# A third weight buffer and one-by-one loads at the start of an MLP, in place of a split store queue and copies on VectorE at its end

## The chip, the cores and the metric

The kernel runs on one core of a Trainium2 chip. A core has five engines that run side by side, each with its own instruction stream: TensorE (PE in the profile) multiplies matrices, VectorE (DVE) and ScalarE (ACT) work element by element, GpSimd (POOL) does the same and issues software transfers, and SyncE (SP) issues most transfers between the off-chip memory (HBM) and the on-chip memory (SBUF). Matmul results land in PSUM, from where VectorE or ScalarE fetch them. An engine executes its instructions in their order: when one of them waits, all behind it wait too. The metric is the device time of one execution in microseconds; lower is better.

## The reference

Attention with a hashed mask, followed by an MLP with a parametric ReLU. There are 4 batches, 8 heads, 768 positions, head size 64; the MLP has 3072 rows, a model size of 512 and a hidden size of 2048. All inputs and outputs are float32.

```python
def _attn_ref(q, k, v, proj):
    q_bits = (np.einsum('bhsd,dk->bhsk', q, proj) > 0).astype(np.int64)
    k_bits = (np.einsum('bhsd,dk->bhsk', k, proj) > 0).astype(np.int64)
    q_bucket, k_bucket = ...            # the 6 bits of each as a number
    mask = q_bucket[:, :, :, None] == k_bucket[:, :, None, :]
    scores = np.where(mask, scale * np.matmul(q, k.transpose(0, 1, 3, 2)), -1e9)
    attn = np.exp(scores - np.max(scores, axis=-1, keepdims=True))
    attn = attn / (np.sum(attn, axis=-1, keepdims=True) + 1e-09)
    return np.matmul(attn, v)

def _moe_ref(x, w_in, w_out, alpha):    # x: attention's output, heads side by side, (3072, 512)
    h = x @ w_in                        # w_in  (512, 2048)
    g = np.maximum(h, 0.0) + alpha * np.minimum(h, 0.0)
    return g @ w_out                    # w_out (2048, 512)
```

## The kernel before

The kernel first runs attention in 32 units (16 pairs of heads, two halves of the queries each). While it does, it rounds the MLP's weights, forms sums of blocks of w_in, and stores both in HBM (w_in_s, w_out_r). Then come 4 batches of the MLP, each with 8 blocks of the first product (called f_0 to f_7) and 7 of the second (z_1, z_2, z_5, z_6, z_3, z_7, z_4, in this order).

Both products use Winograd's form of Strassen's method: seven products of sub-blocks in place of eight, at the price of sums before and after. The class `Product` makes one block. Its steps 1, 2, 22, 5, 6, 3, 7, 4 are seven products in three PSUM banks (a, b, c); `keep` copies a bank to SBUF on ScalarE before more is added on top of it, and `finish` makes a quarter of the result ("11", "12", "22", "21") on VectorE.

```python
    def load_w(n):                       # w_in's blocks for f_n
        if n < B * NI:
            w_m[n] = mid.tile([P, NM, 2, P], F32, name=f"wi{n}", tag="wi")   # the pool has bufs=2
            nc.sync.dma_start(w_m[n], w_in_s[n % NI])

    class Product:
        ...
        def keep(self, bank, what):
            t = mid.tile([P, CW], F32, name=f"{self.name}{what}", tag=what, bufs=1)[:, : self.width]
            do(ACT.copy(t, self.ps[bank]))
            self.sb[what] = t

        def step(self, n):
            if n == 1:
                self.times("a", 0, 0, True)
                self.keep("a", "p1")
            elif n == 2:
                self.times("b", 1, 1, True)
            elif n == 22:
                self.kept("11", self.sb["p1"])
                self.finish("11", self.sb["p1"], self.ps["b"])
            elif n == 5:
                self.times("c", 3, 3, True)
                self.keep("c", "p5")
            elif n == 6:
                self.times("a", 4, 4, False)
                self.keep("a", "u1")
                self.kept("22", self.sb["p5"])
                self.kept("12", self.sb["u1"])
            elif n == 3:
                self.times("c", 6, 2, False)
                self.finish("12", self.sb["u1"], self.ps["c"])
            elif n == 7:
                self.times("a", 5, 5, False)
                self.keep("a", "u2")
                self.finish("22", self.sb["p5"], self.sb["u2"])
            elif n == 4:
                self.times("a", 2, 6, False)
                self.finish("21", self.ps["a"], None)
```

Here `times("a", ...)` of step 6 adds onto bank a, so it has to wait for the copy of p1 that step 1 began. `do` keeps an instruction in program order on its engine; transfers without `do` are placed by the scheduler.

During the first batch, w_out's sums are formed too, 8 groups of them, read from w_out_r and stored to w_out_s by transfers that GpSimd issues:

```python
    def load_out(n):
        if n < NI:
            t = late[0].tile([P, 2, 4, DM // 2], F32, name=f"wo{n}", tag="wl")
            for i in range(2):
                nc.gpsimd.dma_start(t[:, i], w_out_r[:, :, n + i].rearrange("m p d -> p m d"))
                w_o[n + i] = t[:, i]

    def sum_out(n):
        w = w_o[n]
        for to, x, op, y in (...):       # four sums
            do(DVE.tensor_tensor(w[:, to], w[:, x], w[:, y], op=op))
        nc.gpsimd.dma_start(w_out_s[:, :, n].rearrange("m p d -> p m d"), w)
        if n % 2:
            load_out(n + 3)
```

The finished parts of the output are transposed on VectorE and stored (`turn_out`), except the last two parts, which go through TensorE (`turn_last`):

```python
    def turn_out():
        while to_turn:
            ...
            for i in range(2):
                do(DVE.transpose(o[:, :, i], m2[b, p][:, i]))
            for a in range(DM // 128):           # 4
                for c in range(CH):              # 3
                    (nc.scalar if b == B - 1 and p == 3 and c % 2 else nc.sync).dma_start(...)

    def turn_last(n):
        ...
        if n == 0:
            ...                                  # six transposes, two copies on ScalarE, one store
            return
        ps = cells("tx", [(0, 0), (1, 0)])       # TensorE transposes
        ps2 = cells("ty", [(2, 0), (2, 1)])
        do(DVE.tensor_copy(o[:, :, :, 0], ps))
        do(ACT.copy(o2.rearrange("p f i -> p i f"), ps2))
        nc.scalar.dma_start(dst[:, 2], o2.rearrange("p f i -> p (f i)"))
        do(DVE.tensor_copy(o[:, :, :, 1], cells("tz", [(0, 1), (1, 1)])))
        nc.sync.dma_start(dst[:, :2], o.rearrange("p t f i -> p t (f i)"))
```

The loop over the blocks, cut to what the steps need:

```python
    load_out(0)
    load_out(2)
    for j, (b, what, n) in enumerate(blocks):
        ...                                      # steps 2, 22, 5, 6, 3, 7 of this block, and sums for the next
        if j == 4:
            verdict()                            # is every input within the fast path's range?
        for n_out in [(), (0,), (1,), (2,), (3, 4), (5,), (6, 7)][j] if j < 7 else ():
            sum_out(n_out)
        if what == "1":
            load_w(b * NI + n + 2)
            ...
        if j + 1 < len(blocks):
            turn_out()
        else:
            turn_last(0)
        before = now
        if j + 1 < len(blocks):
            now = ...                            # the next block
            now.step(1)
        before.step(4)
        ...
    turn_last(1)
```

Of the kernel before, what the change touches and what calls it, by code (L numbers as in the profile page):

```python
# [406 lines left out]
def fast_path(  # L407
# [59 lines left out]
    qbs = [const.tile([P, S], BF16, name=f"qb{i}") for i in range(2)]  # L467
# [36 lines left out]
    def setup():  # L504

        zero = const.tile([P, 512], BF16, name="zero")
        do(DVE.memset(zero, 0.0))
        do(DVE.memset(wh, 0.0))
        for s in range(2):
            nc.sync.dma_start(wh[D * s : D * s + D, :NB], proj)  # L510
        nc.sync.dma_start(alpha16, moe_alpha.rearrange("(t p) -> t p", p=P))
        make_identity(nc, ident)
        do(DVE.memset(ones, 1.0))

        ps = psum.tile([P, 512], F32, name="nil", tag="av")
        nil.append(lambda: do(PE.matmul(ps, zero[:, :P], zero, start=True, stop=True)))
        for i in range(7):
            nil[0]()

        do(DVE.memset(hb, 0.0))  # L520
        for r in range(0, P, 32):
            do(DVE.memset(hb[r : r + 2 * NB], 1.0 if r % D else -1.0))
            do(DVE.memset(hb[r : r + NB], -1e-37))

        do(DVE.tensor_scalar(hb_k[:, 0:1], hb, -1.0, None, op0=ALU.mult))
        do(DVE.memset(hb_k[:, 1:2], 0.0))
        for r in range(0, P, 32):
            do(DVE.memset(hb_k[r : r + 2 * NB, 1:2], 0.5))
        for t in pts:
            do(POOL.memset(t[:, :, CW : CW + 1], 1.0))  # L530
        for t in qbs:
            do(POOL.memset(t, 0.0))
# [296 lines left out]
    def load_w(n):  # L829

        if n < B * NI:
            w_m[n] = mid.tile([P, NM, 2, P], F32, name=f"wi{n}", tag="wi")
            nc.sync.dma_start(w_m[n], w_in_s[n % NI])

    class Product:
# [3 lines left out]
        def __init__(self, name, width, nk, left, right, finish, kept=None):  # L839
            self.name, self.width, self.nk = name, width, nk  # L840
            self.kept = kept if kept else lambda c, t: None
            self.left, self.right, self.finish = left, right, finish
            self.ps, self.sb = {}, {}
# [21 lines left out]
        def step(self, n):  # L865
# [5 lines left out]
            elif n == 22:  # L871
                self.kept("11", self.sb["p1"])
# [4 lines left out]
            elif n == 6:  # L877
                self.times("a", 4, 4, False)
                self.keep("a", "u1")
                self.kept("22", self.sb["p5"])  # L880
                self.kept("12", self.sb["u1"])
# [56 lines left out]
    def load_out(n):  # L938

        if n < NI:  # L940
            t = late[0].tile([P, 2, 4, DM // 2], F32, name=f"wo{n}", tag="wl")
            for i in range(2):
                nc.gpsimd.dma_start(t[:, i], w_out_r[:, :, n + i].rearrange("m p d -> p m d"))
                w_o[n + i] = t[:, i]

    def sum_out(n):

        w = w_o[n]
# [3 lines left out]
        if n % 2:  # L952
            load_out(n + 3)
# [24 lines left out]
    def ff2(b, n):  # L978
# [11 lines left out]
        def finish(c, x, more):  # L990
            i, jj = int(c[0]) - 1, int(c[1]) - 1
            dst = acc[:, i, jj * HC : (jj + 1) * HC]
            if p == 4:

                do(DVE.tensor_tensor(dst, m2[b, 1][:, i, jj * HC : (jj + 1) * HC] if more is None else dst, x if more is None else more, op=ALU.add))
            elif more is not None:
                do(DVE.tensor_tensor(dst, x, more, op=ALU.add))
            else:
                do(ACT.copy(dst, x))
# [8 lines left out]
        def kept(c, x):  # L1008
            i, jj = int(c[0]) - 1, int(c[1]) - 1
            m = m2[b, 1][:, i, jj * HC : (jj + 1) * HC]  # L1010
            do(DVE.tensor_tensor(acc[:, i, jj * HC : (jj + 1) * HC], x, m, op=ALU.add))

        return Product(
            f"z{b}_{p}", HC, HK, lambda m, k: w2[b, n, m][:, k], lambda m, k: g2[b, n, m][:, k], finish,
            kept if p == 4 else None,
        )

    def turn_out():
        while to_turn:
# [6 lines left out]
            for a in range(DM // 128):  # L1026
                for c in range(CH):
                    cols = slice(half * DM // 2 + 64 * a, half * DM // 2 + 64 * a + 64)

                    (nc.scalar if b == B - 1 and p == 3 and c % 2 else nc.sync).dma_start(  # L1030
# [4 lines left out]
    def turn_last(n):  # L1035


        b, p, half, ch = to_turn.pop(0)
        dst = out_v[b, ch * CH : (ch + 1) * CH].rearrange("c p d -> p c d")[:, :, half * 2 * P : (half + 1) * 2 * P]

        def cells(name, at):
            ps = two_banks(f"{name}{p}")[:, 0].rearrange("p (t f) -> p t f", f=P)
            for k, (t, i) in enumerate(at):
                do(PE.transpose(ps[:, k], m2[b, p][:, i, t * P : (t + 1) * P], ident))
            return ps[:, : len(at)]

        if n == 0:
            o = late[0].tile([P, CH, P, 2], F32, name=f"o_{p}", tag="o")
            for i in range(2):
                do(ACT.copy(o[:, :, :, i], cells(f"to{i}", [(t, i) for t in range(CH)])))  # L1050
            nc.sync.dma_start(dst, o.rearrange("p t f i -> p t (f i)"))
            return
        o = late[0].tile([P, 2, P, 2], F32, name=f"o_{p}", tag="o")
        o2 = late[0].tile([P, P, 2], F32, name=f"o2_{p}", tag="m5", bufs=1)
        ps = cells("tx", [(0, 0), (1, 0)])
        ps2 = cells("ty", [(2, 0), (2, 1)])
        do(DVE.tensor_copy(o[:, :, :, 0], ps))
        do(ACT.copy(o2.rearrange("p f i -> p i f"), ps2))
        nc.scalar.dma_start(dst[:, 2], o2.rearrange("p f i -> p (f i)"))
        do(DVE.tensor_copy(o[:, :, :, 1], cells("tz", [(0, 1), (1, 1)])))  # L1060
        nc.sync.dma_start(dst[:, :2], o.rearrange("p t f i -> p t (f i)"))
# [3 lines left out]
    col = const.tile([32, 32], F32, name="col")  # L1065
    row = const.tile([32, 32], F32, name="row")

    def largest():
        do(DVE.memset(col, 0.0))
# [4 lines left out]
    def verdict():  # L1074
        ps = psum.tile([4, P], F32, name="vd", tag="sm")
        do(PE.transpose(ps, top, ident))
        do(DVE.tensor_reduce(col[:4, 0:1], ps, axis=mybir.AxisListType.X, op=ALU.max))
        do(DVE.transpose(row, col))
        do(DVE.tensor_tensor(row[0:1, 0:1], row[0:1, 0:1], row[0:1, 1:2], op=ALU.mult))

        do(DVE.tensor_scalar(row[0:1, 0:1], row[0:1, 0:1], SAFE, None, op0=ALU.is_le))
        do(DVE.tensor_scalar(row[0:1, 2:3], row[0:1, 2:3], HI_END, None, op0=ALU.is_lt))
        do(DVE.tensor_scalar(row[0:1, 3:4], row[0:1, 3:4], 1.0, None, op0=ALU.is_le))
        do(DVE.tensor_tensor(row[0:1, 0:1], row[0:1, 0:1], row[0:1, 2:3], op=ALU.mult))
        do(DVE.tensor_tensor(row[0:1, 0:1], row[0:1, 0:1], row[0:1, 3:4], op=ALU.mult))
        do(DVE.tensor_scalar(flag, row[0:1, 0:1], -1.0, 1.0, op0=ALU.mult, op1=ALU.add))
# [37 lines left out]
    for u in range(UNITS):  # L1124
# [37 lines left out]
        if u == HW + 2:  # L1162
            load_w(0)
            load_w(1)
            load_x(0)
        if HW + 4 <= u < HW + 8:
            sum_x(0, u - HW - 4, DVE)
# [15 lines left out]
    load_out(2)  # L1183
# [3 lines left out]
    for j, (b, what, n) in enumerate(blocks):  # L1187
# [25 lines left out]
        if j == 4:  # L1213
            verdict()
        for n_out in [(), (0,), (1,), (2,), (3, 4), (5,), (6, 7)][j] if j < 7 else ():
            sum_out(n_out)
        if what == "1":
            load_w(b * NI + n + 2)
# [52 lines left out]
```

## Time and profile before

| | us |
|---|---|
| time, median of 3 runs | 907.64 (906.12 to 910.24) |
| span of the profiled execution | 908.5 |
| attention with the weights' rounding | to about 346 |
| first batch of the MLP | about 346 to 486 |
| batches 2 to 4 | about 135 each |
| end of the last matmul, start of the last store's issue | 900.8, 901.28 |

A line of the profile gives busy time, share of the span and number of instructions of an engine. The chain of waits is followed back from the last instruction, at each step to what released it. The names of the pieces are the program's: `f_2a` is bank a of block f_2, `wi` are w_in's blocks in SBUF, `wl` are w_out's, `m` is a block of the second product's result, `z_4p` is a kept copy of block z_4, `ACTq` and `SPq` are the transfers that ScalarE and SyncE issue. Batch numbers are left out of the names. A busy TensorE is not TensorE at its peak, since matmuls are pipelined. A granted clock below 1 (`PEclk`, in tenths) means that TensorE's pulses were throttled.

### The profile page before, as it was taken

How to read it: one execution, taken by the hardware profiler on the slowest of the kernel's cores; microseconds unless marked ns; L12 is line 12 of the kernel's file. 1: busy time of each engine (PE TensorE's matmuls, PEld its weight loads, DVE VectorE, ACT ScalarE, POOL GpSimd, SP SyncE). 2: the span in 40 equal slices, each digit the busy share in tenths (PEclk: the TensorE clock that was granted, in tenths of full speed). 3: DMA queues.
4: the chain of work that ended last, by engine and by line, in shares of the span. 5: the costliest groups of instructions: out<-in, count | busy, mean ns of one | idle time of the engine just before them, and what ended most of it. 6: DMA issues, size and time to landing. Idle time of an engine off the chain costs nothing.

```text
span 908.5 us, 15657 instructions
## 1 busy us (share of the span) xinstructions
PE 890.3 (98%) x5882; PEld 593.7 (65%) x5882; DVE 755.0 (83%) x1357; ACT 408.6 (45%) x731; POOL 100.6 (11%) x194
## 2 busy tenths in 40 slices
PE   8999999999999999999999999999999999999995
PEld 4444454444444444557997557997557997557994
DVE  4888988988999996799889678898678898678883
ACT  6888888878888862222112222112222112222111
POOL 1222222222222231110000000000000000000000
PEclk9999999999999999999999999999999999999997
DMA  8777888698798574578334434334334434430431
GB/s 221 186 188 184 210 228 210 153 294 217 176 245 213 143 185 163 176 246 302 139 111 120 147 122 151 143 107 129 138 122 151 144 106 124 142 122 1 145 105 56
DMA packets 131909, 146.88 MB, mean 162 GB/s; under 512 B 78304, under 2 KB 118000, under 8 KB 128240
## 3 DMA queue, kind: packets, MB, share of 16 engines
q1 hardware_dynamic: 118496, 124.16, 44.0%
q0 software_dynamic: 11008, 20.97, 11.4%
q8 instruction: 48, 0.79, 0.4%
q10 hardware_dynamic: 2320, 0.66, 0.3%
q14 instruction: 37, 0.30, 0.1%
HBM read 104.87 MB, written 28.31 MB: 147 GB/s over the span
## 4 chain that ended last, share of the span: by engine, by line
PE 91%; DMA 3%; DVE 3%; issue 1%; SPq 0%; ACTq 0%; ACT 0%; DVEq 0%
PE sc L734 17%; PE av L767 14%; PE z_4a L855 2%; PE f_0a L855 2%; PE f_2a L855 2%; PE f_5a L855 2%; PE z_3a L855 2%; PE z_6a L855 2%; PE z_5a L855 2%; PE f_3a L855 2%; PE z_2a L855 2%; PE f_6a L855 2%; PE f_4a L855 2%; PE f_1a L855 2%; PE z_7a L855 2%; PE z_1a L855 2%
## 5 line engine op out<-in xcount | busy, mean ns | idle before, releaser
L739 ACT ACTIVATE pt<-sc 128x768 f32<-128x768 f32 x192 | 152.9, 814 | 46.3 <-PE sc L734 43.9
L734 PE MATMUL sc<-qT,kT 64*128 64x384 f32 x768 | 155.3, 482 | 0.0
L767 PE MATMUL av<-pt,vn 128*32 128x384 f32 (+1 forms) x1536 | 130.6, 488 | 0.0
L767 PEld LDWEIGHTS av<-pt,vn 128*32 128x32 f32 x1536 | 46.6, 109 | 75.1 <-issue 72.1
L734 PEld LDWEIGHTS sc<-qT,kT 64*128 64x128 f32 x768 | 68.2, 188 | 35.1 <-issue 34.8
L908 DVE TENSOR_TENSOR g<-g,g 128x384 f32<-128x384 f32 x128 | 68.4, 555 | 2.2
L734 PE MATMUL sc<-qb,kb 64*128 64x384 bf16 x384 | 63.4, 324 | 2.0 <-ACT kb L722 0.8
L749 POOL DMA_DIRECT2D accp<-pt x32 | 38.6, 1205 | 190.9 <-issue 86.2
L976 DVE TENSOR_TENSOR gs<-g,gs 128x768 f32<-128x768 f32 x56 | 53.4, 953 | 1.0
L968 DVE TENSOR_TENSOR ws<-wl 128x512 f32<-128x512 f32 x56 | 38.5, 688 | 18.7 <-DMA wl<-w_out_s 17.3
L976 DVE TENSOR_TENSOR gs<-g 128x768 f32<-128x768 f32 x56 | 53.3, 953 | 0.0
L904 DVE SCALAR_TENSOR_TENSOR g<-h,alpha 128x384 f32<-128x384 f32 x32 | 19.7, 617 | 27.8 <-ACT h L897 27.8
L734 PEld LDWEIGHTS <-kb 64*128 64x128 bf16 x384 | 19.4, 94 | 33.3 <-issue 11.4
L711 ACT ACTIVATE qb<-hs,hb 32x384 bf16<-32x384 f32 x62 | 35.6, 574 | 1.1
L757 DVE TENSOR_TENSOR accd<-accd,accp 128x768 f32<-128x768 f32 x32 | 30.7, 958 | 4.4 <-DMA accp<-pt 3.4
L754 DVE TENSOR_TENSOR accd<-accd,pt 128x768 f32<-128x768 f32 x32 | 30.7, 958 | 3.3
L748 DVE TENSOR_TENSOR accp<-pt,pt 128x768 f32<-128x768 f32 x32 | 30.4, 951 | 2.6 <-ACT pt L739 2.6
L753 DVE TENSOR_TENSOR accd<-pt,pt 128x768 f32<-128x768 f32 x32 | 30.4, 949 | 0.0
L803 POOL COPY rr<-rr 32x6 f32<-32x6 f32 x64 | 27.6, 432 | 2.6
L722 ACT ACTIVATE kb<-hs,hb 64x384 bf16<-64x384 f32 (+1 forms) x47 | 27.2, 579 | 0.6
L802 POOL COPY rr<-rr 32x6 f32<-32x6 f32 x64 | 19.9, 311 | 65.5 <-DVE rr L799 64.2
L797 DVE STREAM_TRANSPOSE st<-sm 128x192 f32<-128x192 f32 x32 | 12.2, 381 | 15.8 <-PE sm L779 15.7
(349 smaller groups left out, 1826.5 us busy)
## 6 DMA issues: line engine op xcount, KB each, us to landing
wi<-w_in_s SPq DMA_DIRECT2D x32, 896.0 KB, 4.8
wl<-w_out_s SPq DMA_DIRECT2D x16, 1024.0 KB, 4.8
accp<-pt POOLq DMA_DIRECT2D x32, 384.0 KB, 5.6
wl<-w_out_r SPq DMA_DIRECT2D x12, 1024.0 KB, 4.8
raw<-in_moe_w_out_dram SPq DMA_DIRECT2D x16, 512.0 KB, 5.6
raw<-in_moe_w_in_dram SPq DMA_DIRECT2D x16, 512.0 KB, 4.4
w_in_s<-wsi SPq DMA_DIRECT2D x16, 448.0 KB, 5.8
vn<-in_v_dram SPq DMA_DIRECT2D x16, 384.0 KB, 6.0
```

Of the source, the lines that this page charges most:

```text
L711: do(ACT.activation(bits["q", pi][D * s : D * s + 32, cols], ps["q"][c : c + 32, half, :CW], AF.Sign, bias=hb[c : c + 32],))
L734: do(PE.matmul(sc[:, s, :CW], what["k", pi][r, ks], what["q", pi][r, qs], start=first, stop=not first,))
L739: do(ACT.activation(pt[:, :, :CW], sc[:, :, :CW], AF.Exp, scale=SCALE / DOWN))
L748: do(DVE.tensor_tensor(accp[u], p(u, 0), p(u, 1), op=ALU.add))
L749: nc.gpsimd.dma_start(accp[u], p(u, 2), accum_op=ALU.add)
L754: do(DVE.tensor_tensor(accd[u], accd[u], p(u, 5), op=ALU.add))
L757: do(DVE.tensor_tensor(accd[u], accd[u], accp[u], op=ALU.add))
L767: do(PE.matmul(av[u][D * s + t : D * s + t + 32, :w], nat["v", pi][:, s, kc * D + t : kc * D + t + 32], prob[u, kc][:, s, :w], start=(kc = ...
L855: do(PE.matmul(self.ps[bank], self.left(left, k), self.right(right, k), start=start and k == 0, stop=k == self.nk - 1, skip_group_check=no ...
L908: do(DVE.tensor_tensor(new_g(b, to)[:, i], g_m[b, x][:, i], g_m[b, y][:, i], op=ALU.subtract))
L968: do(DVE.tensor_tensor(t, w2[b, n, x], w2[b, n, y], op=op))
L976: do(DVE.tensor_tensor(t, g2[b, n, x], g2[b, n, y], op=ALU.subtract))
```

## The change

w_in's blocks get three buffers, so that a block's weights can be asked for one block earlier; the bits of q and a zero tile move to the pool that ends with attention, which makes room. w_out's groups are loaded one by one, at fixed places of the first five blocks, where the version before loaded them in pairs, each pair from within the sums of an earlier group. In exchange, the change takes out what the version before did at the end: adding quarters of block z_4's kept copies to the result ahead of the matmuls they wait for, splitting the stores of one output part over two queues, and copying the last transposes on VectorE and ScalarE at once. The final range verdict also has another form.

```diff
-    qbs = [const.tile([P, S], BF16, name=f"qb{i}") for i in range(2)]
+    qbs = [pool.tile([P, S], BF16, name=f"qb{i}", bufs=1) for i in range(2)]
...
-            w_m[n] = mid.tile([P, NM, 2, P], F32, name=f"wi{n}", tag="wi")
+            w_m[n] = mid.tile([P, NM, 2, P], F32, name=f"wi{n}", tag="wi", bufs=3)
...
             elif n == 22:
-                self.kept("11", self.sb["p1"])
                 self.finish("11", self.sb["p1"], self.ps["b"])
...
                 self.keep("a", "u1")
-                self.kept("22", self.sb["p5"])
-                self.kept("12", self.sb["u1"])
...
     def load_out(n):
-        if n < NI:
-            t = late[0].tile([P, 2, 4, DM // 2], F32, name=f"wo{n}", tag="wl")
-            for i in range(2):
-                nc.gpsimd.dma_start(t[:, i], w_out_r[:, :, n + i].rearrange("m p d -> p m d"))
-                w_o[n + i] = t[:, i]
+        if n % 2 == 0:
+            w_o[n] = late[0].tile([P, 2, 4, DM // 2], F32, name=f"wo{n}", tag="wl")
+        nc.gpsimd.dma_start(w_o[n - n % 2][:, n % 2], w_out_r[:, :, n].rearrange("m p d -> p m d"))
...
         nc.gpsimd.dma_start(w_out_s[:, :, n].rearrange("m p d -> p m d"), w)
-        if n % 2:
-            load_out(n + 3)
...
-            if p == 4:
-                do(DVE.tensor_tensor(dst, m2[b, 1][...] if more is None else dst, x if more is None else more, op=ALU.add))
-            elif more is not None:
+            if more is not None:
                 do(DVE.tensor_tensor(dst, x, more, op=ALU.add))
+                if p == 4:
+                    add(4, 1, i, jj)
+            elif p == 4:
+                do(DVE.tensor_tensor(dst, x, m2[b, 1][:, i, jj * HC : (jj + 1) * HC], op=ALU.add))
...
-                    (nc.scalar if b == B - 1 and p == 3 and c % 2 else nc.sync).dma_start(
+                    nc.sync.dma_start(
...
     def turn_last(n):
+        goes = [([(t, i) for i in range(2) for t in range(CH)], slice(0, CH))]
+        if n:
+            goes = [([(2, 0), (2, 1), (0, 0), (1, 0)], slice(2, CH)), ([(0, 1), (1, 1)], slice(0, 2))]
+        for cells, ts in goes:
+            ps = two_banks(f"to{p}")...
+            for t, i in cells:
+                do(PE.transpose(ps[:, i, t], m2[b, p][:, i, t * P : (t + 1) * P], ident))
             for i in range(2):
-                do(ACT.copy(o[:, :, :, i], cells(f"to{i}", [(t, i) for t in range(CH)])))
+                t = [c[0] for c in cells if c[1] == i]
+                if t:
+                    t = slice(min(t), max(t) + 1)
+                    do(ACT.copy(o[:, t, :, i], ps[:, i, t]))
+            (nc.scalar if n else nc.sync).dma_start(dst[:, ts], o[:, ts].rearrange("p t f i -> p t (f i)"))
-        ...                              # the two-engine form printed above
...
     def verdict():
-        ps = psum.tile([4, P], F32, name="vd", tag="sm")
-        do(PE.transpose(ps, top, ident))
-        do(DVE.tensor_reduce(col[:4, 0:1], ps, axis=mybir.AxisListType.X, op=ALU.max))
-        do(DVE.transpose(row, col))
+        ps = psum.tile([1, 4, P], F32, name="vd", tag="sm")
+        for n in range(4):
+            do(PE.transpose(ps[:, n], top[:, n : n + 1], ident))
+        do(DVE.tensor_reduce(row, ps, axis=mybir.AxisListType.X, op=ALU.max))
...
+        if u == HW + 9:                  # in attention's loop over units
+            load_w(2)
...
     load_out(0)
-    load_out(2)
...
+        for n_out in [(1,), (2,), (3,), (4, 5), (6, 7)][j] if j < 5 else ():
+            load_out(n_out)
         if what == "1":
-            load_w(b * NI + n + 2)
+            load_w(b * NI + n + 3)
```

## The prediction

> **What bounds the kernel now.** I read the page first, then the list of who waited for whom (TensorE, then VectorE, from the first MLP block to the end), then the chain of waits and the busy windows in the two places where TensorE had waited, and the timeline of the last 30 us.
>
> The page's shares and slices:
>
> ```profile
> span 908.5 us, 15657 instructions
> ...
> PE 890.3 (98%) x5882; PEld 593.7 (65%) x5882; DVE 755.0 (83%) x1357; ACT 408.6 (45%) x731; POOL 100.6 (11%) x194
> ...
> PEclk9999999999999999999999999999999999999997
> ```
>
> TensorE (PE) is busy 98% of the span at full clock, except in the last slice. So only its few idle places are to be had, and the span leaves 18 us in all, of which some 8 lie after the last matmul. The list of TensorE's waits between 345 us and the end names five:
>
> ```profile
> PE z_4a L855 <- ACT z_4p L862: 3.1, 1, 3.1
> PE f_2a L855 <- DMA wi<-w_in_s: 1.8, 1, 1.8
> PE f_7a L855 <- DMA wi<-w_in_s: 1.0, 1, 1.0
> PE f_5a L855 <- DMA wi<-w_in_s: 0.6, 1, 0.6
> PE z_2c L855 <- DVE m L997: 0.2, 1, 0.2
> ```
>
> Columns: who waited for what, total us, times, longest. Three waits are for the first product's weights in the first batch (3.4 us), one is for VectorE just after them, and the longest is in the last block. No wait of this kind exists in batches 2 to 4.
>
> The chain of waits through the first batch (start us, length, what) shows that the weight loads are not all there is:
>
> ```profile
> 354.24 8.17 DMA wi<-w_in_s
> ...
> 362.46 1.56 PE f_2a L855 x4
> ...
> 408.99 0.49 ACT f_6u L862
> 409.50 0.57 DVE f_6p L900
> ...
> 432.30 0.36 DVE m L997
> 432.66 0.04 issue
> 432.71 1.57 PE z_2c L855 x8
> ```
>
> From 409.50 to 432.66 the chain lies on VectorE. The busy windows say the same: VectorE is busy 17.80 of 19.08 us from 390.42 to 409.50, and 22.59 of 23.21 us from 409.50 to 432.71.
>
> The chain near the end:
>
> ```profile
> 887.55 0.96 DVE o L1023 x2
> 888.51 0.02 issue
> 888.53 0.38 ACTq L1030
> ...
> 890.47 0.33 ACT z_4p L862
> 890.80 0.04 issue
> 890.84 2.93 PE z_4a L855 x8
> 893.77 2.56 PE z_4c L855 x8
> ```
>
> Four stores sit in ScalarE's (ACT) own instruction stream ahead of the copy of z_4's first product. ScalarE waits for VectorE's transposes (to 888.5), issues for 1.84 us, and only then copies z_4p, whose matmul had begun at 882.35. TensorE stands from 887.71 to 890.84, and its next products take 2.93 and 2.56 us where the same eight matmuls took 1.30 from start to start before. The windows show the granted clock at 0.50 from 890 to 896 us and 1.00 again from 897.
>
> **What the Trainium skill says.** "TensorE: Matmul & The Clock Gate", section "What's actually happening", says that TensorE's clock falls to half after an idle window of about 3.4 us and comes back after about as much sustained work, the window running free. The trace agrees in kind: a pause of 3.1 us was enough, and half clock lasted some 6 us; the 1.8 us wait at 360.7 left the clock at 1.00. "DMA: Bandwidth & Descriptors", section "Issuing engines are not separate DMA queues", says that stores from several engines share the same 16 DMA engines, so that a second issuing engine saves only sequencer time. Here SyncE issues its eight in 3.70 us and ScalarE its four in 1.84 us, 0.46 us each: the second queue saves 1.84 us of issue that nothing waits for.
>
> **The change, part by part.**
>
> *Third weight buffer.* The compiled order of SyncE's queue puts w_in group 2 right behind groups 0 and 1, in the attention part (they were issued at 192.69 us). After that the same loads leave at the same block ends, each for the group one later: at 354.24 group 3 instead of 2, needed only at 371.6. The three weight waits go. Each also cost the restart: f_2a's group occupied 1.55 us (362.46 to 364.01) against 1.29, so 0.26 more. TensorE alone would gain 1.80 + 0.64 + 0.97 + 3 x 0.26 = 4.2 us. But VectorE takes over. It last waits for TensorE with room to spare at 390.42, before f_5a's wait, so only f_2a's 2.06 us reach it there. From 390.42 to 432.66 it has one gap, 0.46 us at 409.04, which an earlier TensorE closes: 2.06 + 0.46 = 2.5. The after's verdict reduces four rows of 128 on one partition instead of one row on four, and drops a 0.20 us transpose: the old reduction took 0.27 us for 128 elements, so my estimate for 512 is near 0.65, net +0.15 on VectorE. z_2c can start 2.5 - 0.15 = **2.3 us** earlier, not 4.2; TensorE will stand nearly 2 us at z_2a or z_2c instead. A second chain gives the same size: sum_out(7) on VectorE ends near 414.1, its store lands at 423.3, wl_1 is loaded to 428.2, and z_2a starts at 428.29.
>
> *w_out's groups one by one.* GpSimd's (POOL) compiled queue has the same 16 loads and stores in the same order, with the same waits, before and after. In the source the loads of groups 4 and 5 move behind the store of group 2; in the compiled queue they stand ahead of it in both, as the scheduler places them. I count **0**.
>
> *Stores on one queue.* The ScalarE stores go. z_4p is then copied at 883.9, right after its matmul, and TensorE does not stop. From 887.55, at the full-clock durations: z_4a 1.30, z_4c 1.30, z_4a 1.30, six transposes 0.82, last z_4a 1.39, so it ends at 893.66 against 899.91. VectorE must keep up: free at 888.50, two adds of 0.97, one difference 0.95, then six quarter additions at 0.29 from 891.35 to 893.1. It does. Gain **6.25 us**. SyncE's twelve stores last until 888.53 + 12 x 0.46 = 894.05, so the 384 KB store of the next part leaves then instead of 893.25; it is not the last.
>
> *Quarters not added ahead.* Six adds remain six; they change order. The last, on quarter 21, is one add either way. **0**.
>
> *VectorE copies to ScalarE, both last stores on ScalarE.* Before, from the end of m (900.29) to the last store's issue (901.28) was 0.99 us. After, with transposes done at 894.1: a copy of 384 (0.45), a copy of 128 (0.27, estimated from the others), issue 0.36, copy of 256 (0.39), and steps of 0.04, so issue near 895.73, 1.68 us after m's end at 894.05. **Loss 0.7 us**. From the last issue to the end is 908.5 - 901.28 = 7.2 us; the same data go out, so I keep it.
>
> *Cost of group 2 in attention.* DMA share is 1.0 to 1.2 from 185 to 220 us, and 896 KB more come in there, near 3.2 us at 280 GB/s. VectorE waits for the accumulated transfer there already (0.87 and 1.25 us), and at 210.88 its sum ends 1.17 us ahead of the totals' matmul. I allow **+0.4 us** on average.
>
> Sum: -2.3 - 6.25 + 0.7 + 0.4 = -7.45, so 907.64 - 7.5 = 900.1 us.
>
> **The rivals.** (1) The three weight waits vanish whole, 4.2 us and the z_2c wait with them: 898. The wait list speaks for it, VectorE's 97% of the stretch against it. (2) The tail gains nothing, because z_4a waits for another thing ScalarE or VectorE has to do: near 905.5. Against: ScalarE was idle for 7.55 us before z_4p, with only the stores ahead of it. (3) The early wi load collides with attention's saturated stretch and stalls the totals by 2 us or more: 902. For it, the 1.17 us of slack; against it, a lull at 220 to 225 us (DMA share 0.21). (4) Losing the added-ahead quarters and VectorE's copies is the larger effect, as their purpose suggests: 909. For that TensorE would have to have been unhindered before, which the 3.1 us and the half clock deny. (5) A short pause remains at the end and the clock falls anyway: 903.
>
> **Range and chances.** Runs of before spread over 906.12 to 910.24, so a median of few can be off by 1.5 us. Gain at the first blocks 1.8 to 4.5, at the tail 3.5 to 6.5, attention 0 to 2 lost: 897.0 to 904.0 holds it 8 times in 10. Faster by 2% means under 889.5, three times what the waits hold: 0.02. Slower by 2%: 0.02.
>
> **What would show it.** Right: no wait of f_2a, f_5a, f_7a for wi; a wait of 1 to 2 us at z_2a or z_2c for VectorE or wl; PEclk at 1.00 until the last matmul; z_4p's copy within 1 us of its matmul's end; the last store issued on ScalarE about 1.7 us after the last m. Wrong: TensorE waits near 200 to 225 us, or a pause over 3 us in the last block.

## The result, and the profile after

| | us, median (lowest to highest) | executions |
|---|---|---|
| before | 907.52 (906.12 to 910.24) | 6 |
| changed | 902.06 (901.19 to 903.01) | 6 |
| ratio | 0.9936, 95% interval 0.992 to 0.9952 | |

The changed kernel is 5.5 us faster. The prediction was 900.1, with 897.0 to 904.0 as its range. Run again beside the experiments, it took 902.73 against 909.33 (ratio 0.9934, 0.991 to 0.9958).

The page of the profile after, the lines that answer to those of before:

```profile
span 900.1 us, 15656 instructions
...
PE 887.3 (99%) x5885; PEld 591.3 (66%) x5885; DVE 754.5 (84%) x1353; ACT 408.6 (45%) x733; POOL 100.4 (11%) x194
...
PEclk9999999999999999999999999999999999999998
```

TensorE's busy time is 3.0 us shorter although it runs three instructions more (the verdict's transposes). Of about that size is what half clock cost before: the two groups of 2.93 and 2.56 us took 1.30 each at full clock, 2.9 us together. The match is rough: TensorE's busy time differs by 1.6 us between the result and the run `copies` described below (885.7 us), though neither has half clock in the MLP before its last matmul. The list of TensorE's waits from 345 us to the end holds one line where it held five:

```profile
PE z_2a L854 <- DMA wl<-w_out_r: 1.7, 1, 1.7
```

The waits for w_in's blocks are gone, and so is the one for z_4p. One new wait stands at z_2a. The chain of waits through it (start, length, what):

```profile
411.92 9.63 DMA w_out_s<-wo
...
421.62 4.80 DMA wl<-w_out_r
426.42 0.04 issue
426.46 1.58 PE z_2a L854 x8
```

The store of w_out's groups 6 and 7 takes 9.63 us to land, only then is its buffer free for wl_1, and z_2a waits for wl_1. VectorE was close behind as a limit. z_2c needs a sum of VectorE's (m) that ends at 430.14, and starts 0.34 us later, 2.23 us earlier than the 432.71 of before:

```profile
429.79 0.35 DVE L986 TENSOR_TENSOR m<-z_1u,z_1c 128x192 f32<-128x192 f32 x1
...
430.48 1.46 PE L854 MATMUL z_2c<-gs,ws 128*128 128x192 f32 x8
```

The chain in the last block shows eight matmuls every 1.30 us, where before TensorE stood 3.1 us and then took 2.93 and 2.56:

```profile
885.49 1.30 PE z_4a L854 x8
886.79 1.30 PE z_4c L854 x8
888.09 1.30 PE z_4a L854 x8
889.39 0.66 PE to L1032 x6
890.04 1.38 PE z_4a L854 x8
```

Where the 8.4 us between the two profiled spans come from: from the first f_1a to the first z_5a it is 86.54 us before (351.47 to 438.01) and 84.29 after (351.39 to 435.68), 2.25 less. From there to the end of the last sum (m) it is 462.28 before (to 900.29) and 456.14 after (to 891.82), 6.14 less. From the last sum to the end it is 8.21 and 8.28.

### The profile page after: what moved, and what is told of

It reads as the page before. It is cut to its first block, busy times and chain, and to the rows that moved or that the text cites. A ratio compares the mean times of both kernels' runs of the same rounds, so it can differ in the third digit from the quotient of the medians.

```text
span 900.1 us, 15656 instructions
## 1 busy us (share of the span) xinstructions
PE 887.3 (99%) x5885; PEld 591.3 (66%) x5885; DVE 754.5 (84%) x1353; ACT 408.6 (45%) x733; POOL 100.4 (11%) x194
## 4 chain that ended last, share of the span: by engine, by line
PE 92%; issue 3%; DMA 3%; ACT 1%; POOL 1%; DVE 0%; ACTq 0%; POOLq 0%; SPq 0%
PE sc L734 17%; PE av L767 14%; PE z_2a L854 2%; PE f_0a L854 2%; PE z_4a L854 2%; PE z_7a L854 2%; PE z_3a L854 2%; PE z_6a L854 2%; PE z_5a L854 2%; PE f_1a L854 2%; PE f_2a L854 2%; DMA w_out_s<-wo 2%; PE z_1a L854 2%; PE f_7a L854 2%; PE f_6a L854 2%
## 5 line engine op out<-in xcount | busy, mean ns | idle before, releaser
L980 DVE TENSOR_TENSOR m<-m,m 128x768 f32<-128x768 f32 (+1 forms) x36 | 27.1, 752 | 0.7
```

## The experiments

Each kernel was timed beside the kernel before on the same chip. The first four rows are one set, the next four a second, the last four a third; "before beside it" is the same number within a set. Each median is over six executions, except 14 of `again`, 8 of `sponly` and 22 of `wi3`, and 37, 13 and 11 of before in the three sets. "E" stands for the changed kernel with w_out's sums moved earlier (described below). None of these kernels leaves work out.

| run | what it is | median us | before beside it | ratio (95% interval) |
|---|---|---|---|---|
| again | before, unchanged | 909.46 | 909.31 | 1.0003 (0.9989 to 1.0017) |
| sponly | before, all stores on SyncE | 904.49 | 909.31 | 0.9954 (0.9934 to 0.9973) |
| wi3 | before, third weight buffer | 907.58 | 909.31 | 0.9984 (0.9973 to 0.9995) |
| copies | changed, last copies as before | 903.49 | 909.31 | 0.9942 (0.9924 to 0.996) |
| after_again | changed, unchanged | 902.73 | 909.33 | 0.9934 (0.991 to 0.9958) |
| early | E | 898.70 | 909.33 | 0.9894 (0.9872 to 0.9916) |
| pool_sums | changed, sums on GpSimd | 902.72 | 909.33 | 0.9937 (0.9912 to 0.9962) |
| early_tail | E, last copies on two engines | 899.52 | 909.33 | 0.9905 (0.9883 to 0.9927) |
| early_again | E, unchanged | 899.12 | 909.79 | 0.9887 (0.9866 to 0.9909) |
| early_kept | E, quarters added ahead | 899.35 | 909.79 | 0.9888 (0.9867 to 0.9908) |
| early_act1 | E, 384 KB store on ScalarE | 898.85 | 909.79 | 0.9881 (0.9861 to 0.9901) |
| early_act | early_tail and early_act1 in one | 898.38 | 909.79 | 0.9876 (0.9856 to 0.9897) |

### The end: one line, and a clock that falls by chance

The first question was whether 6.25 us, read from one execution, is what the last block loses in every one. `again` is the kernel before, unchanged; `sponly` changes nothing in it but the split of the stores:

```diff
-                    (nc.scalar if b == B - 1 and p == 3 and c % 2 else nc.sync).dma_start(
+                    nc.sync.dma_start(
```

> The kernel before, unchanged, run again. Theory A (the pause of about 3 us in the last block lies at the edge of what TensorE's clock bears, so that the clock falls to half in some executions and not in others): the executions fall into two groups some 2.5 to 3 us apart, and the mean granted clock of an execution is lower in the longer ones (0.994 as in the profiled one of 910.2 us, against 0.997 or more near 907.5). Theory B (the clock falls in every execution): all executions show about 0.994, and the 910.2 us came from elsewhere.

> The kernel before with one edit: the four stores of the last batch's part 3 that ScalarE issued go to SyncE. Theory: the whole gain at the end comes from this line; z_4a no longer waits for z_4p, the last-slice clock stays at 1.00, the profiled span falls by 6 us where the pause had also halved the clock, and the median by 3.3 to 4 us where it had not. Rival (the quarters added ahead and the two engines for the last copies matter as much): under 2 us.

`sponly` took 904.49 against 909.31, 4.8 us less (ratio 0.9954, 0.9934 to 0.9973). Its list of TensorE's waits from 345 us to the end, columns as above:

```profile
PE f_2a L855 <- DMA wi<-w_in_s: 1.9, 1, 1.9
PE f_5a L855 <- DMA wi<-w_in_s: 0.9, 1, 0.9
PE f_7a L855 <- DMA wi<-w_in_s: 0.8, 1, 0.8
PE z_2a L855 <- DMA wl<-w_out_r: 0.6, 1, 0.6
```

The weight waits are all there and z_4a's is gone: the one line is the cause of the pause in the last block. In `again`, the repeat of before, that pause is 3.7 us long. The windows of its last block (start:end us, length, busy us and number of instructions of TensorE, weight loads, VectorE, ScalarE and GpSimd, then granted clock, DMA share, GB/s) show the same picture as before, with less half clock:

```profile
890.00:891.00 1.00, 0.00 (x0) 0.00 (x0) 0.00 (x0) 0.00 (x0) 0.00 (x0) 1.00 0.43 98
...
892.00:893.00 1.00, 1.00 (x4) 1.00 (x4) 0.96 (x2) 0.14 (x1) 0.00 (x0) 0.50 0.43 94
...
895.00:896.00 1.00, 1.00 (x7) 1.00 (x6) 0.90 (x4) 0.00 (x0) 0.00 (x0) 0.82 0.00 0
```

TensorE stands from before 890, then runs 4 or 5 matmuls in a microsecond where it runs 7 or 8 at full clock, for some 4 us instead of more than 6. How much half clock follows is not fixed. The same kernel's execution times go with the mean granted clock of the execution. Of 75 executions of before in the three sets, 26 had a mean clock of 0.997 or more and a median of 907.4 us; 45 had 0.995 or less and a median of 910.3. (It is a slope more than two separate groups: the six lowest, at 0.991 and 0.992, took 911.7 to 913.4.) `sponly` has the same two groups: five at 0.997 or more with a median of 904.4, two at 0.995 or less at 906.5 and 906.7 (one at 0.996 took 903.5). So within a group the line is worth 3.0 to 3.7 us, near the bare pause with its restart (3.13 + 0.26 = 3.4), and by the difference of the groups, an estimate, half clock adds some 2 to 3 us to those executions that get it. Where it fell in the executions without a profile is not shown. The split by mean clock is a rough one: the mean also counts the drop of the clock after the last matmul (0.50 at 895 us in the result), and the profiled execution of `again` counts 0.997 and still has the short stretch above.

### The weights: what stood behind the three waits

`wi3` does the other half alone: before, with three buffers for w_in.

```diff
-    qbs = [const.tile([P, S], BF16, name=f"qb{i}") for i in range(2)]
+    qbs = [pool.tile([P, S], BF16, name=f"qb{i}", bufs=1) for i in range(2)]
...
-            w_m[n] = mid.tile([P, NM, 2, P], F32, name=f"wi{n}", tag="wi")
+            w_m[n] = mid.tile([P, NM, 2, P], F32, name=f"wi{n}", tag="wi", bufs=3)
...
+        if u == HW + 9:
+            load_w(2)
...
-            load_w(b * NI + n + 2)
+            load_w(b * NI + n + 3)
```

(The zero tile moves to `pool` in the same way.)

> The kernel before with the third buffer for the first product's weights alone (and what makes room for it), w_out's groups still loaded in pairs. Theory: the three waits of f_2a, f_5a and f_7a go (4.2 us with their restarts), but 1.7 to 2 us come back as a wait at z_2a or z_2c, so the gain is 2.3 us, 905.2 where before is 907.5; the waits at the end stay. Rival 1 (loading one by one is what moves the wait): the wait at z_2a is absent or much larger here than in the changed kernel. Rival 2: the gain is the whole 4.2 us.

It took 907.58 against 909.31, 1.7 us less (0.9973 to 0.9995). With the 4.8 of `sponly` that makes 6.5, and the whole change gave 6.6 in its repeat (902.73 against 909.33): the two parts account for it, as closely as intervals of 1 to 2 us to either side can tell. The waits of `wi3`:

```profile
PE z_4a L855 <- ACT z_4p L862: 3.1, 1, 3.1
PE z_2a L855 <- DMA wl<-w_out_r: 2.1, 1, 2.1
PE z_1c L855 <- DVE f_7u L900: 0.2, 1, 0.2
```

The wait at z_2a is there although w_out's groups are still loaded in pairs. So the one-by-one loading does not cause it; it is what the weight waits had hidden (before's and `sponly`'s profiles have it small, 0.2 us at z_2c and 0.6 at z_2a). This run also holds both of TensorE's pauses in one execution, and the clock does the opposite of what their lengths suggest (columns as in the windows above):

```profile
428.00:429.00 1.00, 1.00 (x5) 1.00 (x4) 0.97 (x2) 0.32 (x1) 0.00 (x0) 0.50 0.91 342
...
430.00:431.00 1.00, 1.00 (x5) 1.00 (x4) 1.00 (x4) 0.24 (x1) 0.00 (x0) 0.50 0.00 0
...
889.00:890.00 1.00, 0.00 (x0) 0.00 (x0) 0.00 (x0) 0.22 (x2) 0.00 (x0) 1.00 0.65 137
...
891.00:892.00 1.00, 1.00 (x8) 1.00 (x7) 0.96 (x2) 0.19 (x1) 0.00 (x0) 1.00 0.29 66
```

After the 2.1 us at z_2a the clock is at 0.50 from 428 us to near 432; after the 3.1 us at z_4a it stays at 1.00. With the clock halved there, the stretch from the first f_1a to the first z_5a is 86.19 us in `wi3`, though its 3 waits are gone.

The repeat of the whole change met the same:

> The changed kernel, unchanged, run again. Theory (a pause of 1.7 to 2 us at z_2a lies where TensorE's clock sometimes falls to half): most executions near 902 with a mean clock of 0.997 or more, some 2 to 3 us longer with 0.994 to 0.996. Rival: no execution shows the lower clock, because the pause is too short.

Its profile has a 2.2 us wait at z_2a and half clock behind it, and the stretch takes 86.47 us, where the profile of the result, with 1.7 us and no half clock, has 84.29. Of its six executions two have a mean clock of 0.995 or 0.996 and take 904.3 and 904.7; the other four take 901.4 to 903.3. That is what the expectation said.

If the store of groups 6 and 7 holds wl_1 back, moving w_out's sums and loads earlier must remove the wait. E does so, in the changed kernel:

```diff
-        for n_out in [(), (0,), (1,), (2,), (3, 4), (5,), (6, 7)][j] if j < 7 else ():
+        for n_out in [(), (0, 1), (2, 3), (4,), (5,), (6, 7)][j] if j < 6 else ():
             sum_out(n_out)
-        for n_out in [(1,), (2,), (3,), (4, 5), (6, 7)][j] if j < 5 else ():
+        for n_out in [(1, 2, 3), (4, 5), (6, 7)][j] if j < 3 else ():
             load_out(n_out)
```

> The changed kernel with w_out's sums one or two blocks earlier, where VectorE has slack: groups 0 and 1 after block 1, 2 and 3 after block 2, then 4, 5, and 6 and 7 after block 5 (before: after block 6), loads moved up with them. The same instructions in all. Theory (what held TensorE at z_2a was VectorE's backlog and the store of groups 6 and 7 that wl_1's buffer waits for): the 1.7 us wait at z_2a and its restart go, about 2 us faster than the changed kernel, and with no pause left the clock stays up, so the executions lie closer together, near 900. Rival (transfers were the bound, and they take what they take): the wait moves to another load and the time stays.

E took 898.70 against 909.33 (ratio 0.9894, 0.9872 to 0.9916), and 899.12 in its repeat; that is 4 us below the changed kernel, twice what was expected. wl_1 is issued at 406.54 instead of 421.62, and the list of TensorE's waits from 345 us to the end is empty. Windows of the repeat of the change first, then of E:

```profile
410.00:427.00 17.00, 15.37 (x71) 11.68 (x69) 16.55 (x31) 3.19 (x8) 1.52 (x2) 1.00 0.85 310
427.00:440.00 13.00, 12.42 (x66) 12.42 (x67) 10.23 (x17) 1.62 (x6) 0.00 (x0) 0.87 0.45 174
```

```profile
410.00:427.00 17.00, 17.00 (x89) 14.76 (x88) 16.65 (x29) 3.83 (x10) 0.00 (x0) 1.00 0.60 218
427.00:440.00 13.00, 13.00 (x82) 12.95 (x81) 11.33 (x19) 2.24 (x7) 0.00 (x0) 1.00 0.48 163
```

TensorE is busy for all 30 us and gets through 171 instructions instead of 137. The first f_1a to the first z_5a takes 81.87 us, 4.67 less than before: the whole of the waits with their restarts, which the change alone could not have. Beside the result's profile it is 2.42 us less, beside the repeat's with its half clock 4.60; between the two lie the 4 us. No execution of the 36 of E and the kernels built on it below has a mean clock under 0.997, and all lie between 897.4 and 900.8 us, where before spreads over 8 us. With the pauses gone, so is this spread.

`pool_sums` asked whether VectorE's load as such was the limit, by giving w_out's sums to GpSimd in the changed kernel:

```diff
-            do(DVE.tensor_tensor(w[:, to], w[:, x], w[:, y], op=op))
+            do(POOL.tensor_tensor(w[:, to], w[:, x], w[:, y], op=op))
```

> The changed kernel with w_out's 32 sums computed by GpSimd in place of VectorE, at the same places. It takes 14 us of work (32 x 0.45) off VectorE between 360 and 415 us. Theory A (VectorE's backlog alone delays the stores and z_2c): VectorE is no longer full from 390 to 430 us, z_2a's wait goes, 2 us faster. Theory B (the store of groups 6 and 7 is what binds): GpSimd's sums are slower, so the store leaves as late or later, and z_2a waits for wl_1 as long as before or longer, though VectorE has time to spare.

Neither theory held whole. It took 902.72, the same as the changed kernel. The wait at z_2a is gone, as theory A had it, but wl_1 is also issued earlier (402.89 us instead of 421.62), against theory B, so the run cannot tell the two apart. Other waits stand in the place of z_2a's: two for VectorE's part of the verdict and two for w_in's blocks, of which the last (0.4 us at f_7a) is left out here:

```profile
PE f_5b L854 <- DVE row L1053: 1.0, 1, 1.0
PE f_6a L854 <- DMA wi<-w_in_s: 0.8, 1, 0.8
PE vd L1052 <- DVE top L1045: 0.7, 1, 0.7
```

VectorE got rid of the sums and was busier until 390 us all the same: 39.80 of the 45 us from 345 to 390, where it was busy 35.09 in the changed kernel. Only from 390 to 430 us had it more room (33.14 of 40 us against 38.62). Groups from 354 to 398 us (line, engine, operation, out<-in, count | busy us, mean ns | idle before): VectorE's sums of g in the changed kernel first, then the same in `pool_sums`, then GpSimd's sums there (350 to 400 us):

```profile
L904 DVE TENSOR_TENSOR g<-g,g 128x384 f32<-128x384 f32 x20 | 10.7, 555 | 0.3
```

```profile
L904 DVE TENSOR_TENSOR g<-g,g 128x384 f32<-128x384 f32 x20 | 17.6, 902 | 0.3
```

```profile
L944 POOL TENSOR_TENSOR wo<-wo 128x256 f32<-128x256 f32 x32 | 28.1, 883 | 4.3 <-DMA wo<-w_out_r 2.8
```

The same twenty sums on VectorE take 902 ns instead of 555 while GpSimd works beside it, and GpSimd needs 883 ns for a sum that VectorE does in 422. The Trainium skill ("GPSIMD Engine Reference", section "1. Specifications") says that GpSimd shares its SBUF interfaces with VectorE, and names VectorE's instructions with two SBUF inputs among those that contend; these sums are such, and the measurement agrees in kind. That the sharing is the reason was not tested by itself. So this run does not tell whether VectorE alone would have been the limit; it tells that moving the sums to GpSimd gains nothing here.

### The last copies and stores

The prediction charged 0.7 us for copying the last transposes on ScalarE alone. `copies` puts the two-engine form of before back into the changed kernel:

```diff
-            for i in range(2):
-                t = [c[0] for c in cells if c[1] == i]
...
-            (nc.scalar if n else nc.sync).dma_start(dst[:, ts], o[:, ts].rearrange("p t f i -> p t (f i)"))
+        ps = cells("tx", [(0, 0), (1, 0)])
+        ps2 = cells("ty", [(2, 0), (2, 1)])
+        do(DVE.tensor_copy(o[:, :, :, 0], ps))
+        do(ACT.copy(o2.rearrange("p f i -> p i f"), ps2))
+        nc.scalar.dma_start(dst[:, 2], o2.rearrange("p f i -> p (f i)"))
+        do(DVE.tensor_copy(o[:, :, :, 1], cells("tz", [(0, 1), (1, 1)])))
+        nc.sync.dma_start(dst[:, :2], o.rearrange("p t f i -> p t (f i)"))
```

> The changed kernel with the last part's copies and stores as in the kernel before: VectorE copies two of the three pieces, SyncE issues the last store. Theory: the last store is issued 1.0 us after the last sum instead of 1.85, so 0.7 to 0.9 us faster than the changed kernel, 901.2 where that is 902.1. Rival (the store's own landing sets the end, and it lands later on SyncE's queue: 256 KB took 4.1 us there): no change.

903.49 against 909.31 (0.9924 to 0.996) is no gain over the changed kernel. Four of its six executions have a mean clock of 0.996 and take 903.3 to 903.9, the other two 900.9 and 902.1, so the chance of the clock blurs the comparison here. The timeline of its end (start, length, what, and in brackets the time stood before and what ended it) shows why it could not gain:

```profile
890.62 0.36 DVE L990 TENSOR_TENSOR m<-z_4a,m 128x192 f32<-128x192 f32 x1 [0.21 <-PE z_4a L854]
...
892.88 0.42 DVE L1043 COPY o<-tx 128x256 f32<-128x256 f32 x1 [1.90 <-DMA out_dram<-o]
```

VectorE's copy waits 1.90 us for its buffer, which the twelve stores of the part before still read. With those on one queue they end later, so the last store leaves at 893.66, 2.68 us after the last sum instead of the 1.0 of the theory, and the two-engine form loses what it was for. So this run did not test what an earlier last store is worth. `early_tail` is the same form on E with a buffer of its own for all three stripes (the diff is against the form above):

```diff
-        o = late[0].tile([P, 2, P, 2], F32, name=f"o_{p}", tag="o")
-        o2 = late[0].tile([P, P, 2], F32, name=f"o2_{p}", tag="m5", bufs=1)
+        o = late[0].tile([P, CH, P, 2], F32, name=f"o_{p}", tag="m5", bufs=1)
```

> The kernel with the earlier sums, and the last part's copies again on VectorE and ScalarE with the last store on SyncE, now into the buffer that m5 leaves, so that nothing waits for the twelve stores (the run with the old copies showed a 1.9 us wait of VectorE for them). Theory: the last store is issued about 1.0 us after the last sum, 0.7 to 0.9 us earlier than with ScalarE alone, so 0.7 us faster than the run with earlier sums alone. Rival: the landing of the stores ahead of it sets the end, and nothing is won.

The wait is gone and the last store is issued 0.98 us after the last sum's end, against 1.80 in E. The time is 899.52 against E's 898.70: no gain is seen from 0.8 us at the last issue.

`early_kept` adds before's quarters, added ahead, to E (with before's `finish` for block z_4, left out here):

```diff
             elif n == 22:
+                self.kept("11", self.sb["p1"])
                 self.finish("11", self.sb["p1"], self.ps["b"])
...
                 self.keep("a", "u1")
+                self.kept("22", self.sb["p5"])
+                self.kept("12", self.sb["u1"])
```

> The kernel with the earlier sums, and with z_4's quarters added ahead again, as in the kernel before. Theory (six adds remain six and the last one, on quarter 21, is alone behind the last matmul in both): no change, within 0.3 us. Rival (adding ahead takes adds off the path that sets the end): faster by 0.35 us for each add taken off, up to 1 us.

> The kernel with the earlier sums, run again beside the next three, which differ from it in one thing each. Expected near 898.7, executions within 1.5 us of each other.

899.35 beside 899.12 for E in the same set (whose executions lie 2.5 us apart, wider than the 1.5 expected): no difference is seen from the order of the quarters, with a TensorE that does not stop.

What does set the end? The 384 KB store of the part before the last was issued behind the twelve on SyncE. In the profile after, its data were ready near 891.0 and it left at 892.51, right behind them:

```profile
886.85 5.56 SPq L1016 DMA_DIRECT2D out_dram<-o  x12
...
892.51 0.40 SPq L1038 DMA_DIRECT2D out_dram<-o  x1
892.83 0.37 ACTq L1038 DMA_DIRECT2D out_dram<-o  x1
...
893.66 0.39 ACTq L1038 DMA_DIRECT2D out_dram<-o  x1
```

The stores from 885 us on of E, printed below, land within 1 us of one another: 889.05 + 4.5, 889.37 + 4.5 and 890.20 + 4.3 us. `early_act1` moves the 384 KB store to ScalarE's queue in E; `early_act` does so in `early_tail`:

```diff
-            (nc.scalar if n else nc.sync).dma_start(dst[:, ts], ...)
+            nc.scalar.dma_start(dst[:, ts], ...)
```

> The kernel with the earlier sums, and the 384 KB store of the part before the last on ScalarE's queue, so that it doesn't wait on SyncE for the twelve small stores ahead of it. Theory (the end is set by the three last stores' data, 768 KB that leave in a bunch because the first of them is held up 1.5 us behind the twelve): the 384 KB leave 1 us or more earlier, the last store lands in nearer 3 than 4.3 us, 0.7 to 1 us faster. Rival (the last store's issue alone sets the end): no change, or 0.3 us slower for the issue on ScalarE.

> As the run before this one, with the last part's copies on VectorE and ScalarE too and its last store on SyncE. Theory: with the 384 KB out of the way the earlier last issue counts, so 0.5 to 0.8 us faster than with the store on ScalarE alone, near 897.3. Rival: the landing of the bunch still sets the end, no further gain.

The stores from 885 us on (KB each, median us from issue to landing), E first, then `early_act`:

```profile
out_dram<-o SPq DMA_DIRECT2D x1, 384.0 KB, 4.5
...
out_dram<-o ACTq DMA_DIRECT2D x1, 256.0 KB, 4.3
out_dram<-o ACTq DMA_DIRECT2D x1, 128.0 KB, 4.5
```

```profile
out_dram<-o ACTq DMA_DIRECT2D x1, 384.0 KB, 2.9
...
out_dram<-o SPq DMA_DIRECT2D x1, 256.0 KB, 3.1
out_dram<-o ACTq DMA_DIRECT2D x1, 128.0 KB, 1.9
```

In `early_act` the large store leaves 1.06 us before the last sum's end instead of 0.65 after it, and all three stores take less time to land. But the last issue is no earlier than E's, 1.87 us after the last sum against 1.80, though its copies end as early as in `early_tail`. SyncE waits for an earlier store to land (engine and line, what it waits for, us, times, longest):

```profile
SPq L1046 <- DMA out_dram<-o: 1.7, 1, 1.7
```

It leaves at 890.89, when the 384 KB store, issued at 887.96 with 2.9 us to land, has landed. So the theory of `early_act`, an earlier last issue with the 384 KB out of the way, was not put to the test. The time is 898.85 for `early_act1` and 898.38 for `early_act` beside 899.12 for E: 0.3 and 0.7 us, less than expected, and the three intervals overlap (0.9881, 0.9861 to 0.9901; 0.9876, 0.9856 to 0.9897; 0.9887, 0.9866 to 0.9909). The order in the traces is shown; that it makes the kernel faster is not. `early_act` has the lowest median of all the kernels. The executions of E and of the kernels built on it (at most 900.8 us) all lie below those of the changed kernel (901.2 and more) and of before.

## Why the prediction was right or wrong

**First batch, -2.3.** Right in size and in reason. The three waits went, and f_1a to z_5a became 2.25 us shorter in the profile; z_2c starts 2.23 us earlier, where 2.3 was worked out. Of the two chains that the prediction gave as the next limit, the chain of waits names the second: store of groups 6 and 7, wl_1, z_2a. E moved that work earlier and the rest of the 4.7 us came. It moved VectorE's sums too, and `pool_sums` moved both chains, so no run takes one chain away alone. The result's trace says how near the first was: VectorE is busy 19.52 of the 20 us from 410 to 430, so the sum that z_2c needs could have come at most some 0.5 us earlier, and z_2c starts 0.34 us after it. By this estimate z_2c could have gained less than 1 us without the wait for wl_1. The 2.3 was summed on VectorE's chain alone; that the other chain, which the prediction gave without a sum, came out within 1 us of it was luck. What was missing from this step is that the clock can halve after the new 2 us wait, which in two of the four profiles that have it (`wi3` and the repeat, not `copies` and the result) took nearly the whole gain back.

**w_out's groups one by one, 0.** Right as far as is seen: `wi3`, with pairs, has the same wait, and its stretch of 86.19 us is no worse than the 86.47 of the changed kernel's repeat, both with half clock behind the wait.

**Stores on one queue, -6.25.** The mechanism was right: no pause, full clock to the last matmul, and 6.14 us less from the first z_5a to the last sum in the two profiles. As a difference of medians it was too large. The step took a pause and some 6 us of half clock from one profiled execution and counted both in full. The line alone gave 4.8 us between medians (`sponly`), of which by the groups of mean clock some 3.4 come in every execution and the rest only where the clock falls. The baseline adds to it: 907.64, the median of three executions from which the whole 6.25 was taken off, is near the upper-clock group (907.4), while the profiled execution among them, from which the 6.25 was read, took 910.24 at a mean clock of 0.994.

**Copies on ScalarE, +0.7.** The step failed. The last issue did come later, 1.84 us after the last sum against 0.99 (1.68 was worked out). But from the last sum to the end it was 8.28 us against 8.21, because the 7.2 us from the last issue to the end, which the step kept as they were, became 6.4. The last store's landing is only 0.2 us of that (901.28 + 4.1 before, 893.66 + 3.9 after). The rest lies behind the landing, where no transfer of the output and no computation is left: some 3.0 us before, 2.5 after. It is 2.9 us or more in the four profiles of before and its variants and 2.5 or less in the ten of the changed kernel and its variants, `early_kept`, `copies` and `early_tail` among them; so neither the quarters nor the last copies make it, and the third buffer (`wi3`: 3.5) doesn't either. What does, the verdict's new form or another part, was not tested. In `early_tail` no gain is seen from an earlier last issue. The traces show the last three stores landing as a bunch when the 384 KB one is held behind the twelve; that this is why the last issue does not set the end is argued, not shown. One profile each varies by about 1 us in this piece (8.60, 8.28, 7.48 and 7.61 in four kernels of the E family whose last copies are alike), so 0.7 us is below what it can show.

**Group 2 in attention, +0.4.** Not found. TensorE has no wait from 185 to 235 us and the first f_1a starts at 351.39 against 351.47. The lull at 220 to 225 us took the backlog: its DMA share rose from 0.21 to 0.64.

**Quarters not added ahead, 0.** Right as far as is seen: `early_kept`, 899.35 beside 899.12.

The sum was 7.45 and 5.5 came; beside the experiments, with more executions of before, 6.6. Without the two charges that were not found the sum would have been 8.55. Against that the runs put 4.8 where the prediction had 6.25, and 1.7 where it had 2.3, together 2.05 less. Most of that is, as far as the groups of mean clock tell, the difference between a stretch at half clock counted in full and one that comes by chance, at the end and at z_2a. The other 1.1 us between 6.6 and 5.5 is before's own median, 907.5 in one set and 909.3 in the other, less the 0.7 by which the changed kernel differed. Rival (1), the whole 4.2 us, was false for the change and true for E; rivals (2) and (3) have no wait in the profile after to stand on; against rival (4) stand `early_kept`, `copies` and `early_tail`, where neither the quarters nor VectorE's copies made the kernel faster; rival (5), a pause that lowers the clock, happened, but at z_2a and not at the end.

## What to carry to other kernels

Four stores put into the queue of ScalarE, which also copies for TensorE, held the copy behind them until the stores' data were there, and TensorE with it for 3.1 to 3.7 us; put such stores where nothing is behind them. A pause of TensorE of 2 to 4 us cost some 2 to 3 us more through the clock here, in some executions and not in others, so read how long the pause is and how often the clock falls before taking one trace's loss as the gain. And when a wait for a load is removed, follow what the next buffer is waiting for: here the third buffer was worth some 2 us, and two lines of the schedule another 4.

## What the runs showed of the hardware

- The prediction expected the clock to go by the length of the pause. Pauses of 2.1 us (`wi3`), 2.2 us (the repeat of the change), 3.1 us (before) and 3.7 us (`again`) were followed by half clock; one of 3.1 us (`wi3`), one of 1.9 us (`copies`) and one of 1.7 us (the result) were not. The Trainium skill ("TensorE: Matmul & The Clock Gate", section "What's actually happening") gives about 3.4 us of idle and a window that runs free; the free-running window agrees with the chance, the length does not agree with the pauses of 2.1 to 3.1 us, and the measurement stands.
- GpSimd's two-input sums took 883 ns on average for 128x256 against VectorE's 422, and VectorE's sums of g, 128x384, beside them 902 ns instead of 555. The longest sum of VectorE's there, of f_1p with 128x384, took 2246 ns, where it took 557 in the changed kernel.
- A 384 KB store took 2.6 to 2.9 us to land when it left about a microsecond before the last sum's end (before, `early_act1`, `early_act`), and 4.1 to 4.5 when it left 0.7 us after it, within 1.2 us of the last two stores (the result, E). `early_tail` and `copies`, where it left 0.3 and 0.4 us after the sum, have 3.1 and 4.5.
- In `early_act` the last store, issued by SyncE, waited 1.7 us until the 384 KB store issued by ScalarE had landed; where both were on SyncE's queue (`early_tail`), it left 0.73 us after the other, before that one had landed. Why the one waits and the other does not, the runs do not show.
